# Making and broadcasting the gate rows at 38000 instead of 24000 of the plan's clock, in a fused attention and mixture kernel

## The chip, the cores and the metric

The kernel runs on one core of one Trainium2 chip. The metric is the time of one execution in device microseconds (us); before the change the median of three runs is 361.21 us.

## The reference

Two stages follow each other. Attention with four sink keys and a window of 128 keys runs over 4 batches, 8 heads, 768 positions of width 64. Its output, laid out as 3072 tokens of width 512, is the input of four experts, and every token goes through all of them, weighted by its gate:

```python
# _attn_ref, cut
scores = scale * np.matmul(q, k.transpose(0, 1, 3, 2))
keep = is_sink | in_window
a = softmax(np.where(keep, scores, -1e9))
x = np.matmul(a, v)            # -> (3072, 512)
# _moe_ref, cut
p = domain_probs / (domain_probs.sum(-1, keepdims=True) + 1e-09)
for e in range(E):
    h = np.maximum(x @ w1[e], 0.0)
    out += p[:, e:e + 1] * (h @ w2[e])
```

The shapes are w1 (4, 512, 1024), w2 (4, 1024, 512) and the probabilities (3072, 4).

## The kernel before, in words

**Tiles.** Each batch has three groups of 256 positions (g = 0, 1, 2). Attention goes by batch, group and head pair: transposes or DMA transposes of q and k, scores (L684), exponentials on ScalarE (L709), masks on VectorE (L718 in batch 0, L703 later), products with the values (L743 for the sinks, L750 for the window), a reciprocal and a scaling (L777, L780 or L789), and in batch 0 a transpose back (L808) into `xT`. The experts take `xT` group by group. A unit is (batch, group, expert).

**Two ways for a unit.** A slow unit has four steps of eight matmuls in its first layer (L1058). A fast one has seven products P1 to P7 of combined blocks (L1145), for which VectorE forms sums and differences of the weights (`vf` from w1 at L377 to L383, `wf` from w2 at L341 to L347) and of the tokens (L1114), and between the products VectorE and ScalarE combine partial results (L1191, L1198, L1204, L1213).

**Where the gates come in.** The units of batch 0's groups 0 and 1 are "early" units: ScalarE or VectorE evicts the first layer with a plain maximum (L1071, L1073), the second layer is L1397, and the gate is applied as one number for each token when VectorE evicts it (L1407, L1409). These numbers, `scale_t`, are made from the probabilities by `gates()` (L908 to L913), apart from the code changed here. Every later unit multiplies the gate in when its first layer is evicted (L1082 for slow units, L1178 for fast ones); there the tokens lie along the free dimension, so the gate must lie as a row, the same in all 128 partitions. The second layer of these units is L1319.

**Making the rows.** `gates_by_row()` (from L433) normalises the probabilities on VectorE with 24 partitions (L434 to L437), and SyncE (SP) stores the result in DRAM with two DMAs (L441). `load_gates()` (from L446) then lets SP broadcast rows from there to all partitions, 128 KB each, into at most NGATE = 5 buffers (L457): five at once, each further one when a buffer's unit is finished. The probabilities and the rows lie in `scratch` (L424), whose memory later takes `vf` of expert 2.

```python
    def gates_by_row():                                             # L433
        nc.vector.reduce_sum(out=ds, in_=dp, axis=AX.X)
        nc.vector.tensor_scalar_add(out=ds, in0=ds, scalar1=1e-9)
        nc.vector.reciprocal(out=ds, in_=ds)
        nc.vector.tensor_mul(
            pn, dp.rearrange("n p e -> n e p"), ds[:, None, :].to_broadcast([NT, E, P]),
        )
        for i in range(2):
            nc.sync.dma_start(out=gate_rows[:, :, i, :], in_=pn[i:NT:2])
        dve(2800, 0.0)
```

**What sets the order.** The instructions are issued by a planner that runs when the program is built. It keeps a clock for each engine in estimated ns (`t["pe"]`, `t["dve"]` and so on), and in each turn of its loop (L1455) emits the piece of TensorE work that is ready soonest or has the best priority; evictions and other work of VectorE and ScalarE wait in a list with due times and are emitted when their engine's clock allows. Every engine then carries out its own instructions in that order, and waits by semaphores for what they need. `now` is TensorE's clock. The call of the gate rows stands at the head of the loop, ahead of the turn's other emissions:

```python
        if not rowed and now > ROWED:                               # L1461
            rowed = 1
            gates_by_row()
            load_gates()
```

`dve(2800, 0.0)` puts the chain's estimate of some 3 us on VectorE's clock. The landing of a gate is in no clock of the planner. If no gate has been asked when the first gated unit opens, `emit_first` (L1033) asks for them itself; such units open only after attention of batch 0 is issued.

**The loads.** The weights of the four experts, 1 MB of DMA writes for each w1 and w2, and the rows of q, k and v go by GpSimd's (POOL's) queue, in the order of a list: w1 and w2 of expert 0, the last rows of batch 0, then w1 and w2 of experts 1 and 2, w1 of expert 3, rows of batch 1, w2 of expert 3 (L312, L322, L234, L299). SP's queue has the first loads, the gate rows, the DMA transposes (L246, L767) and the stores of the output.

Of the kernel before, what the change touches and what calls it, by code (L numbers as in the profile page):

```python
# [16 lines left out]
def kernel(  # L17
# [63 lines left out]
    OPEN = 2.2  # L81
    SOON = 21000
    NEARLY = 2
    ROWED = 24000
    W2AT = 2
    ROWS1 = 1500
    ONACT = 1
# [1367 lines left out]
    while mix.more() or att.more():  # L1455
        now = t["pe"]

        if not att.more() and ahead == B - 1 and not wide:
            wide = 1
            mix.widened()  # L1460
        if not rowed and now > ROWED:  # L1461
            rowed = 1
# [107 lines left out]
```

## Time and profile before

| | before |
|---|---|
| median of 3 runs | 361.21 us (360.98 to 362.25) |
| profiled execution, span | 361.5 us |
| around the span | nothing listed |
| TensorE (PE) busy | 351.5 us, 97% |
| VectorE (DVE) busy | 303.8 us, 84% |
| ScalarE (ACT) busy | 162.4 us, 45% |
| GpSimd (POOL) busy | 71.7 us, 20% |
| DMA moved | 37.79 MB, mean 105 GB/s |
| granted TensorE clock | 0.999 |
| gate chain on VectorE (L434) | starts at 24.9 us |
| first five gate broadcasts (L457) | issued from 34.7 us |
| first gated eviction (L1082) | 53.4 us |

The profile is one execution, so its rows are compared with its own span. Two kinds of line need a word. A line of a waits view names the engine and line that waited, what released it, and then total us, number of times and the longest. PE is TensorE's matmuls and PEld its weight loads, which overlap them. The DMA share of the page is full until about 135 us and low after that, so the first third of the run and the rest have different limits.

### The profile page before, as it was taken

What the parts mean: (1) busy time and instruction counts of PE and PEld (TensorE: products, weight loads), DVE (VectorE), ACT (ScalarE), POOL (GpSimd) and SP (SyncE); (2) the same over time, 40 slices, a digit from 0 to 9 for tenths busy, and PEclk for the clock granted to TensorE, in tenths of its full rate; (3) what the DMA queues carried; (4) which work ended last, traced back from release to release, by engine and by line L of the source; (5) the groups of instructions that cost most, each with busy time, mean ns of one, the idle gap of its engine ahead of it and who ended that gap; (6) DMA issues with size and microseconds to landing.
All of it is one profiled execution on the core that took longest, in us unless ns stands there. A gap on an engine that the chain in (4) does not pass through costs nothing.

```text
span 361.5 us, 10704 instructions
## 1 busy us (share of the span) xinstructions
PE 351.5 (97%) x4476; PEld 302.4 (84%) x4484; DVE 303.8 (84%) x691; ACT 162.4 (45%) x414; POOL 71.7 (20%) x92
## 2 busy tenths in 40 slices
PE   8999989998999999999999999999999999999995
PEld 3575758766789898898899898899899999999984
DVE  6787969868799899699579999989879799899840
ACT  5854722447694373554544435345344432313110
POOL 8936012540356224001071000000000000000000
PEclk9999999999999999999999999999999999999999
DMA  9999999999999999217099712121310131110011
GB/s 165 171 180 194 232 210 180 156 146 169 176 133 173 162 157 135 61 47 86 19 158 173 126 65 55 31 75 16 60 62 28 31 76 60 31 58 4 3 60 59
DMA packets 117869, 37.79 MB, mean 105 GB/s; under 512 B 100676, under 2 KB 113316, under 8 KB 117820
## 3 DMA queue, kind: packets, MB, share of 16 engines
q0 software_dynamic: 77520, 17.31, 54.0%
q1 hardware_dynamic: 39244, 19.28, 27.8%
q8 instruction: 35, 0.57, 0.6%
q10 hardware_dynamic: 1056, 0.52, 0.5%
q14 instruction: 14, 0.11, 0.1%
HBM read 40.98 MB, written 6.34 MB: 131 GB/s over the span
## 4 chain that ended last, share of the span: by engine, by line
PE 86%; DMA 11%; DVE 1%; issue 1%; ACT 1%; POOL 0%; ACTq 0%; POOLq 0%; DVEq 0%
PE acc L1319 34%; PE cps L1145 32%; DMA w<-in_moe_w_dram 9%; PE hps L1058 7%; PE acc L1397 6%; PE sps L684 3%; PE od L750 2%; DMA kraw<-in_k_dram 2%; PE od L743 1%; PE sinks L645 0%; ACT aT L709 0%; POOL w L312 0%; DVE qkn L345 0%; DVE qkn L343 0%; ACT qkn L270 0%
## 5 line engine op out<-in xcount | busy, mean ns | idle before, releaser
L1145 PEld LDWEIGHTS <-w 128*128 128x128 bf16 x1184 | 72.5, 98 | 2.3 <-issue 0.9
L1319 PEld LDWEIGHTS <-H 128*128 128x128 bf16 x700 | 65.0, 98 | 8.0 <-issue 1.5
L1178 DVE SCALAR_TENSOR_TENSOR H<-cps,gates 128x512 bf16<-128x512 f32 x90 | 60.3, 679 | 0.1
L709 ACT ACTIVATE aT<-sps 128x512 bf16<-128x512 f32 (+1 forms) x96 | 46.9, 573 | 24.7 <-PE sps L684 24.6
L1319 PE MATMUL acc<-w,H 128*128 128x256 bf16 x420 | 55.4, 273 | 0.0
L1145 PEld LDWEIGHTS <-vf 128*128 128x128 bf16 x744 | 45.6, 98 | 1.2 <-issue 0.5
L1145 PE MATMUL cps<-T,w 128*128 128x128 bf16 x592 | 45.0, 219 | 0.0
L1058 PE MATMUL hps<-xT,w 128*128 128x256 bf16 x352 | 43.3, 273 | 0.9 <-DMA w<-in_moe_w_dram 0.9
L1145 PE MATMUL cps<-xT,w 128*128 128x128 bf16 x592 | 43.7, 219 | 0.0
L789 ACT ACTIVATE onat<-od,R 128x64 bf16<-128x64 f32 x144 | 33.2, 323 | 22.7 <-DVE R L777 22.6
L1191 ACT COPY cps<-cps 128x512 f32<-128x512 f32 x37 | 21.4, 578 | 42.1 <-PE cps L1145 27.5
L1058 PEld LDWEIGHTS <-w 128*128 128x128 bf16 x352 | 33.3, 98 | 6.6 <-DMA w<-in_moe_w_dram 1.2
L1369 ACT COPY osb<-acc 128x256 f32<-128x256 f32 x36 | 13.6, 377 | 50.7 <-PE acc L1319 50.7
L1145 PE MATMUL cps<-T,vf 128*128 128x128 bf16 x496 | 36.4, 219 | 0.0
L299 POOL DMA_DIRECT2D vx<-in_v_dram x24 | 21.6, 905 | 62.2 <-PE od L750 48.5
L1319 PEld LDWEIGHTS <-S 128*128 128x128 bf16 x320 | 30.4, 98 | 3.3 <-issue 0.2
L1397 PE MATMUL acc<-w,H 128*128 128x512 bf16 x120 | 29.3, 379 | 2.0 <-DMA w<-in_moe_w_dram 1.3
L1198 DVE TENSOR_TENSOR cps<-H,cps 128x512 f32<-128x512 f32 x32 | 22.1, 691 | 9.8 <-PE cps L1145 8.4
L1319 PE MATMUL acc<-wf,H 128*128 128x256 bf16 x208 | 29.3, 273 | 0.0
L703 DVE TENSOR_TENSOR aT<-aT,mask 128x1024 bf16<-128x1024 bf16 (+1 forms) x36 | 22.7, 640 | 4.3 <-ACT aT L709 4.0
L1213 DVE TENSOR_TENSOR H<-H,cps 128x512 f32<-128x512 f32 x32 | 21.8, 680 | 2.7 <-PE cps L1145 2.6
L1397 PEld LDWEIGHTS <-H 128*128 128x128 bf16 x128 | 12.1, 98 | 13.5 <-issue 1.7
(128 smaller groups left out, 546.2 us busy)
## 6 DMA issues: line engine op xcount, KB each, us to landing
w<-in_moe_w_dram POOLq DMA_DIRECT2D x7, 1024.0 KB, 18.3
out_dram<-osb SPq DMA_DIRECT2D x21, 256.0 KB
gates<-gate_rows SPq DMA_DIRECT2D x40, 128.0 KB
vx<-in_v_dram POOLq DMA_DIRECT2D x24, 128.0 KB, 7.0
qkn<-in_q_dram POOLq DMA_DIRECT2D x22, 128.0 KB, 8.8
qkn<-in_k_dram POOLq DMA_DIRECT2D x22, 128.0 KB, 9.8
w<-in_moe_w_dram POOLq DMA_DIRECT2D x2, 512.0 KB, 9.4
kraw<-in_k_dram ACTq DMA_DIRECT2D x2, 256.0 KB
```

The costliest lines, as they stand in the source:

```text
L299: nc.gpsimd.dma_start(out=vx[tb][:, :, 0:D], in_=v[b, :, tb * P:(tb + 1) * P, :].rearrange("h p d -> p h d"),)
L703: nc.vector.tensor_mul(a, a, m[:, None, :].to_broadcast([P, 2, w]))
L709: nc.scalar.activation(out=a[:, ph], in_=sps[ph][:, 0:w], func=AF.Exp, scale=scale)
L789: nc.scalar.mul(o[:, qi, hp, ph * D:(ph + 1) * D], od[:, qi, ph, 0:D], R[:, qi, ph])
L1058: nc.tensor.matmul(h[:, i].rearrange("p (q n) -> p q n", q=2), lhsT=w1_sb[e][:, db, fb * P:(fb + 1) * P], rhs=xT[b, g][:, :, db], start=(i ...
L1145: nc.tensor.matmul(y[:, f], lhsT=A[:, d, f * P:(f + 1) * P], rhs=T[:, d], start=(m in ("P1", "P5") and f == 0 and d == 0), stop=(d == 1), ...
L1178: nc.vector.scalar_tensor_tensor(out=dst, in0=src, scalar=0.0, in1=gate, op0=ALU.max, op1=ALU.mult)
L1191: nc.scalar.copy(out=tiles["Y"], in_=y)
L1198: nc.vector.tensor_add(tiles["V"], c5, tiles["X"])
L1213: nc.vector.tensor_add(c5, c5, y)
L1319: nc.tensor.matmul(x, lhsT=self.operand(b, g, e, m)[:, f], rhs=forms[e][m][:, f], start=(k == 0 and f == 0 and m in (("P1", "P5", "P2") if ...
L1397: nc.tensor.matmul(op, lhsT=H[:, fb // QF, fb % QF, s], rhs=w2_sb[e][:, fb, :], start=(fb == 0), stop=(fb == NFB - 1),)
```

## The change

One constant of the planner changes. The gate rows are made, stored and broadcast in the first turn of the loop in which TensorE's clock has passed 38000 instead of 24000. No operation is added or removed by the edit itself; VectorE's clock gets the chain's estimate at the later point, and what the planner emits after either point may come in another order. In the trace of before the two stores are issued ahead of the DMAs that ask for expert 2's weights (28.8 and 29.7 us on POOL).

```diff
     OPEN = 2.2
     SOON = 21000
     NEARLY = 2
-    ROWED = 24000
+    ROWED = 38000
     W2AT = 2
     ROWS1 = 1500
     ONACT = 1
```

## The prediction

> **What bounds the kernel now.** I read four things in this order: the page's first part, the idle time of TensorE by cause, the timeline round the gates, and the DMA traffic in the same stretch.
>
> ```profile
> PE 351.5 (97%) x4476; PEld 302.4 (84%) x4484; DVE 303.8 (84%) x691; ACT 162.4 (45%) x414; POOL 71.7 (20%) x92
> ```
>
> TensorE is the bound: 351.5 of 361.5 us. Of the 10 us left, 3.3 lie in the first 20 us (busy 16.68) and 3.8 after 340 us (busy 17.75 of 21.5), mostly behind the last product. The waits of PE name what the edit can reach:
>
> ```profile
> PE acc L557 <- DVE lent L468: 1.4, 1, 1.4
> PE acc L1397 <- DMA w<-in_moe_w_dram: 1.3, 1, 1.3
> PE hps L1058 <- DMA w<-in_moe_w_dram: 0.9, 1, 0.9
> PE sinks L645 <- DVE qkn L345: 0.8, 1, 0.8
> ```
>
> The second is the one beside the gates: a second layer (L1397) waits for expert 1's w2. The timeline has both:
>
> ```profile
> 24.94 0.67 DVE L434 TENSOR_REDUCE scratch<-scratch 24x128 f32<-24x512 f32 x1
> 26.87 1.07 DVE L437 TENSOR_TENSOR scratch<-scratch 24x512 f32<-24x512 f32 x1
> 27.96 1.72 SPq L441 DMA_DIRECT2D gate_rows<-scratch  x2
> 34.66 2.28 SPq L457 DMA_DIRECT2D gates<-gate_rows  x5
> 46.21 1.89 PE L1397 MATMUL acc<-w,H 128*128 128x512 bf16 x7 [1.32 <-DMA w<-in_moe_w_dram]
> 53.36 0.69 DVE L1082 SCALAR_TENSOR_TENSOR H<-hps,gates 128x512 bf16<-128x512 f32 x1 [0.40 <-PE hps L1058]
> ```
>
> Columns: start, us, engine, line, operation; in brackets the idle time before. The chain of four DVE operations runs 24.94 to 27.94, the first broadcast is issued at 34.66, w2 of expert 1 is there at 46.17, and no gate is read before 53.36. The waits of SP's queue between 25 and 62 us give the latencies:
>
> ```profile
> SPq L457 <- DMA gate_rows<-scratch: 4.9, 1, 4.9
> SPq L457 <- DMA gates<-gate_rows: 3.1, 1, 3.1
> ```
>
> From DVE's end (27.94) to the first broadcast's issue is 6.7 us, 4.9 of them spent on the landing of the stores. The five issues end at 36.94, and 3.1 us later (40.07) the first gate is in: 5.4 us after its issue. The DMA answers for 35 to 38 us, 38 to 46 us and 46 to 53 us, in that order (packets, MB, share):
>
> ```profile
> q0 software_dynamic: 588, 0.62, 123.0%
> ...
> q0 software_dynamic: 832, 1.21, 83.3%
> q1 hardware_dynamic: 719, 0.66, 31.1%
> ...
> q0 software_dynamic: 1237, 1.46, 120.8%
> ```
>
> q0 carries the weights, q1 the broadcasts. Alone, q0 moves 0.62/3 = 0.207 and 1.46/7 = 0.209 MB per us; beside the gates 1.21/8 = 0.151. The gates take 8 x 0.208 - 1.21 = 0.45 MB of weights out of that stretch, 2.2 us of the stream.
>
> **The change part by part.** The plan's clock passed 24000 just before L434, at 24.94. It is TensorE's work that moves that clock, and TensorE idles about 0.4 us in the next 14, so 38000 falls near 24.9 + 14.0 + 0.4 = 39.3 us, between the masks and scalings (L718, L777, L780) of batch 0's last heads.
>
> *Taken away at 25 us:* 3.0 us of DVE and 1.7 us of SP issues. TensorE is busy 19.71 of 20 us there, and the DVE operation that followed (L910) waited 0.82 us for TensorE anyway. Gain: 0, at most 0.2.
>
> *Taken away between 32 and 46 us:* two 24 KB stores and five broadcasts. w2 of expert 1 lands 2.2 us earlier by the bytes: 44.0. By the landings: the weight before it landed at 22.48 + 15.2 = 37.7, and the last of the three after 46.17 at 30.53 + 30.6 = 61.1, so 5.0 each, which gives 37.7 + 5.0 = 42.7. TensorE asks at 46.21 - 1.32 = 44.89, perhaps a microsecond sooner in the new order. The whole wait goes: -1.3 us. What is late next: no wait of TensorE on a transfer follows it.
>
> *Put in at 39.3 us, DVE:* the chain, 0.67 + 0.21 + 0.94 + 1.07 with gaps, 3.0 us, until 42.3. Queued behind it are the remaining R, onat and mask operations of batch 0, and TensorE's L808 and L750 wait for those. The plan books the chain on its DVE clock, so it will put first-layer groups (L1058, evicted by ACT) there: five of 0.87 us run between 39.1 and 44.9, 4.4 us, more than 3.0. So 0 on TensorE. Without that cover it is up to 3.0, and the stretch has DVE idle for only 0.24 us of 39 to 46. The backlog runs on into 46 to 53.4, where DVE is busy 4.21 of 7.4 us: 3.2 idle, enough for 3.0. DVE thus comes to the first gated eviction at about 53.4, as before.
>
> *Put in at 42.3 us, SP:* two stores and then five broadcasts. SP issues nothing else between 8.4 and 60 us, so they are moved past nothing on SP. On POOL the loads of experts 2 and 3 and batch 1's first rows (28.79 to 38.8) are now asked ahead of them; they were queued without waiting for SP, so no issue moves. Repeating the latencies: 42.3 + 6.7 = 49.0 for the first broadcast, 49.0 + 5.4 = 54.4 for the first gate. The other four are wanted from 62.16 (L1178) on and follow over 6 us.
>
> *The wait that this adds:* L1082 has to wait until 54.4, from 53.4: +1.0 on DVE. Queued behind it are expert 2's forms (L377 to L383), the evictions L1409 and, from 59 on, the first fast units (L1198, L1178, L1213), whose next products wait for DVE. DVE idles 0.6 us in 53.4 to 60 and 0.1 in 60 to 67 (busy 6.90 of 7.00), so 1.0 - 0.6 = 0.4 us is left when the fast units run, and there TensorE can't be ahead of DVE: the 1.3 us gained at 45 are handed back, and it leaves this stage 0.4 us, say 0.3 for the last 0.1 idle, later than before. After 67 DVE has 3.5 us of slack in 13.
>
> No trace shows the latencies at the new place. The lower end takes the nearest shorter row for the stores' landing, 3.1 in place of 4.9 us: first gate at 52.6, in time, nothing added. The upper end is both latencies stretched by half, (6.7 + 5.4) x 1.5 = 18.2, first gate at 60.5. I take the measured sum, since weights fill q0 in both stretches alike (0.207 and 0.209).
>
> [...]
>
> *The buffer:* the probabilities lie where vf of expert 2 is written (L377, 53.97). The stores have read them by 49.0; 5 us of cover, cost 0.
>
> *The broadcasts at their new time* slow q0 by the same 2.2 us between about 52 and 61, after w2 of expert 2. What lands later than 61 is where it was. Cost 0.
>
> *The order after 45 us.* The plan redraws it, since its DVE clock differs. It can win at most the 0.8 us wait at 89 us: TensorE is busy 20.00 of 20 in every such window from 120 to 340. It can lose where DVE is full, 19.97 of 20 between 100 and 120: at most the 3.0 moved. I take 0, since the 3.5 us of DVE slack after 67 lie between.
>
> **The sum:** -1.3 + 1.6 (DVE's lag taking TensorE from 1.3 early to 0.3 late) = +0.3 us on the profiled 361.5. The page gives nothing around the span, which lies 0.3 above the runs' median of 361.21 and inside their 360.98 to 362.25; the same +0.3 on the median is 361.5.
>
> **The rivals.** (1) *The gates come in time.* For: 53.4 against 54.4 is one microsecond of difference in a sum of two latencies; against: both latencies were measured beside the same stream. Then the 1.3 us stay won: 359.9, and 359.1 where the 0.8 wait at 89 us goes too. [...]
>
> (2) *The gates are much too late, the slower side.* Place: the first L1082. Price: landing time less 53.4, less 0.7 us of DVE idle until 67. For: the broadcasts now meet the loads of batch 1's short rows, and DVE may enter the chain late, being full from 39 on. Against: the latencies above. It decides from a landing of 55.9 us on, where the loss reaches 1.8; at 57.5 it is 3.4: 364.6.
>
> (3) *The redrawn order pushes DVE work into 100 to 120 us.* For: no idle time there; against: the slack at 67 to 80. +1 to +3.0: 362.2 to 364.2.
>
> (4) *Nothing moves:* a fallback that loads gates when a unit opens could come first. Units open only after batch 0's attention is issued, behind 38000, so hardly: 361.2.
>
> **How the numbers follow.** This measurement can tell 0.5%, 1.8 us. My forecast (-0.6 to +1.4) has 0.42, rival 1 0.24, rival 2 0.18, rival 3 0.13, rival 4 0.03. Faster by more than 1.8 us needs rival 1 with its second wait: 0.10. Slower: all of rival 2, 0.09 of rival 3, 0.05 of the forecast's own upper tail: 0.32. Within: 0.58. The range goes from 359.7 (rival 1 with its one wait) to 364.3 (rival 2 almost to 57.5, and all of rival 3); outside lie about 0.12 below and 0.08 above.
>
> **What would show it.** L434 near 39 us, L441 near 42, L457 near 49; no wait of L1397 for a weight at 45 us; an idle of about 1 us on DVE ahead of the first L1082, put down to the gates' transfer, and TensorE pausing in L1145 at 60 to 67 us. Wrong if the gates are in before DVE asks, if L1397 still waits for its weight, or if TensorE has new idle time after 80 us.

## The result, and the profile after

The change makes the kernel slower: 364.45 us (median of five runs, 363.33 to 365.72) against 361.21 (five runs, 360.93 to 362.69), a ratio of 1.0079 with a 95% interval of 1.0054 to 1.0103, so by less than 1% but clear of the noise. The profiled execution has a span of 363.0 us and took 364.66 us, so 1.7 us lie around the span; the same 1.7 us stand in every later run.

The first part of the page of the changed kernel, engine, busy us, share and instructions, has hardly moved:

```profile
PE 352.8 (97%) x4475; PEld 303.8 (84%) x4483; DVE 303.8 (84%) x688; ACT 163.3 (45%) x417; POOL 71.5 (20%) x92
```

TensorE's busy time is 1.3 us more than in the first profile of before; a second profile of that kernel, below, has 352.5, so little of this is the change's. The waits of PE in the changed kernel (who waited, for what, total us, times, longest) have a new first line, and both waits for weights are gone:

```profile
PE cps L1145 <- DVE H L1082: 2.1, 1, 2.1
PE acc L557 <- DVE lent L468: 1.4, 1, 1.4
```

The timeline of the changed kernel shows the chain, the stores, the broadcasts and the first reader at their new places:

```profile
38.78 0.67 DVE L434 TENSOR_REDUCE scratch<-scratch 24x128 f32<-24x512 f32 x1
40.70 1.07 DVE L437 TENSOR_TENSOR scratch<-scratch 24x512 f32<-24x512 f32 x1
41.80 1.73 SPq L441 DMA_DIRECT2D gate_rows<-scratch  x2
43.07 1.89 PE L1397 MATMUL acc<-w,H 128*128 128x512 bf16 x7
47.84 14.61 SPq L457 DMA_DIRECT2D gates<-gate_rows  x6
55.16 0.69 DVE L1082 SCALAR_TENSOR_TENSOR H<-hps,gates 128x512 bf16<-128x512 f32 x1 [3.78 <-DMA gates<-gate_rows]
62.15 1.16 PE L1145 MATMUL cps<-T,vf 128*128 128x128 bf16 x16 [2.05 <-DVE H L1082]
```

L1397 has no bracket: expert 1's w2 was in at 40.93 by the landing records, 5.2 us sooner than in the profile of before. Not all of that is the gates' doing. The trace has sixteen landing records of this transfer; in the profile of before fifteen are in by 42.62 and the last only at 46.17, and expert 2's two weights behind it have a like lag of 2.7 and 2.6 us in their last record. A second profile of before, below, has w2 in at 43.81. Ahead of L1082 VectorE sits idle for 3.78 us, put down to the gates' transfer; from 60.10 on, 5 us after it starts, TensorE pauses for 2.05. The stores took 41.80 to 47.8, 6.0 us, and the broadcast 47.84 to 55.06, 7.2. SP's queue, from 25 to 62 us, waits 4.3 us for the stores (4.9 before) and, with its five issues done, 5.0 for the first gate (3.1 before):

```profile
SPq L457 <- DMA gates<-gate_rows: 5.0, 1, 5.0
SPq L457 <- DMA gate_rows<-scratch: 4.3, 1, 4.3
```

The chain of the changed kernel, cut to 38 to 64 us (start, us, what), runs from the chain on VectorE through both transfers to the product that paused:

```profile
40.70 1.07 DVE scratch L437
...
42.76 5.02 DMA gate_rows<-scratch
...
47.84 7.23 DMA gates<-gate_rows
...
55.16 0.13 DVE H L1082
...
62.15 1.91 PE cps L1145 x23
```

In the DMA traffic of the changed kernel (packets, MB, share) the first line is 38 to 46 us, where q0 moved 1.21 MB before; the other two are 53 to 60 us, where the broadcasts on q1 now lie:

```profile
q0 software_dynamic: 1139, 1.66, 115.7%
...
q0 software_dynamic: 4174, 0.90, 141.9%
q1 hardware_dynamic: 593, 0.53, 28.6%
```

So the weights did get their stretch back: 1.66 MB in 8 us is the undisturbed 0.208 per us. It bought no time, as the experiments show.

The windows of the changed kernel hold one more thing. Columns: window, length, busy us and count of PE, PEld, DVE, ACT, POOL, then the granted TensorE clock:

```profile
60.00:62.00 2.00, 0.10 (x2) 0.00 (x0) 2.00 (x4) 0.57 (x1) 1.83 (x3) 1.00 2.24 166
62.00:64.00 2.00, 1.85 (x25) 1.84 (x25) 2.00 (x5) 0.58 (x1) 1.79 (x3) 0.74 1.36 203
64.00:66.00 2.00, 2.00 (x22) 2.00 (x21) 1.83 (x4) 0.60 (x1) 1.21 (x2) 0.50 1.22 214
66.00:68.00 2.00, 2.00 (x35) 2.00 (x34) 1.95 (x4) 0.60 (x2) 0.00 (x0) 0.91 1.34 199
```

From 0.8 us after the pause the clock stands at half for 3.41 us (from 62.96 by the clock's records). The third window has 22 products; the same window of a later profile of this kernel at full clock (e6, below) has 34. Half of 3.41 is 1.7 us of TensorE's time.

### The profile page after: what moved, and what is told of

It reads as the page before. It is cut to its first block, busy times and chain, and to the rows that moved or that the text cites. A ratio compares the mean times of both kernels' runs of the same rounds, so it can differ in the third digit from the quotient of the medians.

```text
span 363.0 us, 10702 instructions
## 1 busy us (share of the span) xinstructions
PE 352.8 (97%) x4475; PEld 303.8 (84%) x4483; DVE 303.8 (84%) x688; ACT 163.3 (45%) x417; POOL 71.5 (20%) x92
## 4 chain that ended last, share of the span: by engine, by line
PE 84%; DVE 6%; DMA 5%; ACT 2%; issue 1%; POOL 1%; DVEq 0%; SPq 0%; ACTq 0%
PE acc L1319 33%; PE cps L1145 31%; PE hps L1058 8%; PE acc L1397 5%; PE sps L684 3%; PE od L750 2%; DMA gates<-gate_rows 2%; DMA gate_rows<-scratch 1%; DMA vx<-in_v_dram 1%; ACT aT L709 1%; PE od L743 1%; DVE onat L780 1%; DVE H L1082 1%; DVE H L1178 1%; DVE aT L718 1%
## 5 line engine op out<-in xcount | busy, mean ns | idle before, releaser
L1145 PEld LDWEIGHTS <-w 128*128 128x128 bf16 x1184 | 73.7, 99 | 2.3 <-issue 0.9
L1145 PEld LDWEIGHTS <-vf 128*128 128x128 bf16 x744 | 46.0, 98 | 4.0 <-issue 3.4
L1145 PE MATMUL cps<-T,w 128*128 128x128 bf16 x592 | 46.0, 221 | 0.0
L1145 PE MATMUL cps<-xT,w 128*128 128x128 bf16 x592 | 44.1, 220 | 0.0
L1058 PE MATMUL hps<-xT,w 128*128 128x256 bf16 x352 | 42.9, 273 | 0.0
L1145 PE MATMUL cps<-T,vf 128*128 128x128 bf16 x496 | 36.3, 219 | 2.5 <-DVE H L1082 2.1
L1058 PEld LDWEIGHTS <-w 128*128 128x128 bf16 x352 | 33.4, 98 | 5.0 <-issue 0.6
L1397 PE MATMUL acc<-w,H 128*128 128x512 bf16 x120 | 29.2, 379 | 0.6 <-issue 0.3
L1397 PEld LDWEIGHTS <-H 128*128 128x128 bf16 x128 | 12.1, 98 | 12.1 <-issue 0.2
```

Of the source, the lines that this page charges most:

```text
L1058: nc.tensor.matmul(h[:, i].rearrange("p (q n) -> p q n", q=2), lhsT=w1_sb[e][:, db, fb * P:(fb + 1) * P], rhs=xT[b, g][:, :, db], start=(i ...
L1145: nc.tensor.matmul(y[:, f], lhsT=A[:, d, f * P:(f + 1) * P], rhs=T[:, d], start=(m in ("P1", "P5") and f == 0 and d == 0), stop=(d == 1), ...
L1397: nc.tensor.matmul(op, lhsT=H[:, fb // QF, fb % QF, s], rhs=w2_sb[e][:, fb, :], start=(fb == 0), stop=(fb == NFB - 1),)
```

## The experiments

Theory A was the prediction's own account with the measured latencies: the late gates cost more than foreseen, while w2 wins 1.3 us back. Theory B, formed after the first four runs, says that the wait for w2 was never part of the usual execution. A third candidate was the redrawn issue order. Ratios are against the kernel before, run on the same chip.

**One half of the change alone (e1_split).** The rows are made and stored at 24000 as before; only the broadcasts come at 38000. A small write by VectorE into each new buffer goes with it.

```diff
+        x = mo.tile(...); len(gate_sb) < NGATE and nc.vector.memset(x[:, 0, 0:1], 0.0)
...
             gates_by_row()
-            load_gates()
+        if rowed == 1 and now > 38000: rowed = 2; load_gates()
```

> The chain and the stores stay at 24000, and every engine keeps its order of before; only the first five broadcasts are held back until 38000, by five one-column memsets on VectorE that they have to wait for. Theory (the landing of the gates decides): broadcasts issued near 39.5 us, first gate in near 45, expert 1's w2 in by 43 to 44, so neither the wait of L1397 at 45 us nor a wait of L1082 for a gate: 359.5 to 360.0, faster than before by 1.2 to 1.7 us. Rival (the redrawn order, not the landing, made the change slow, and the weight's wait is not the gates' doing): as before, 361.2, with the wait of L1397 still there.

Measured: 362.11 us, ratio 1.0013 [0.9989, 1.0037]. The first gate was in at 44.58, w2 at 42.53, L1397 did not wait, the first L1082 ran at 51.03 without waiting for a gate. The conditions of a gain of 1.3 us were all met, and no gain came. Four of the ten runs had a mean granted clock of 0.995 and took 363.7 to 363.9 us; the other six took 361.3 to 362.2, level with the 361.86 of before and not 1.3 below it. The longest wait that the edit could have caused is 1.8 us of L645 for a DMA transpose at about 87 us, where the kernel before, run again below, waits 1.0; so up to 0.8 us of a gain could hide there, not the whole.

**The order of before, the chain late (e2_plan_of_before).** The planner's clock is charged at 24000 as before, and chain, stores and broadcasts are issued at 38000, unbooked.

```diff
-        dve(2800, 0.0)
...
-            gates_by_row()
-            load_gates()
+            dve(2800, 0.0)
+        if rowed == 1 and now > 38000: rowed = 2; gates_by_row(); load_gates()
```

> The chain, the stores and the broadcasts stand at 38000 as in the change, but the plan books them at 24000, so all other work keeps its order of before. Theory (landing): first gate in near 55 us as in the change; VectorE comes to L1082 later than in the change (near 53.4 instead of 51.4), so it waits 1 to 2 us instead of 3.8, and TensorE also waits up to 2 us near 40 to 45 because nothing was planned to cover the chain: 361.5 to 363.5. Rival (the redrawn order is what costs): back to 359.8 to 361.2.

Measured: 364.24 us, ratio 1.0049 [1.0031, 1.0067]; chain at 39.91, stores 42.9, broadcasts 48.98, first gate 54.76. Here the chain itself stops TensorE, as its timeline shows:

```profile
43.48 0.28 PE L808 MATMUL tx<-ident,onat 128*128 128x128 bf16 x2 [2.61 <-DVE onat L780]
```

The first L1082 comes only at 55.43 and waits 0.40 us for its own product, not for a gate, so theory A's wait of 1 to 2 us there did not come. Of the 4.4 us that it is later than in the kernel before (51.00 in the second profile, below), 2.6 are this hold-up; 1.7 are a wait of L1058 for a weight near 20 us, ahead of the chain, which belongs to this execution and not to the edit. The 3.0 us of chain thus hold TensorE up by 2.6 where the plan does not book them. In the change, where it does, TensorE's longest wait for L780 is 0.2, since it has first-layer products to do, as a line of the changed kernel's timeline shows:

```profile
38.71 4.53 PE L1058 MATMUL hps<-xT,w 128*128 128x256 bf16 x40
```

So the cover by first-layer groups is real, and the change pays at the gates instead. In time the hold-up of e2 comes to less than 2.6: the four other runs at a clock of 1.0 took 362.9 to 363.3 us, 1.0 to 1.4 above before, and the five at 0.995 took 364.1 to 364.6.

**The first gate not loaded (e3_first_gate_set).** The change, but GpSimd sets the first buffer to 1.0 where SP would load it, which leaves out the gating of that one unit and 128 KB of broadcast; the order on VectorE and TensorE is that of the change.

```diff
-        nc.sync.dma_start(
+        nc.gpsimd.memset(x, 1.0) if not gate_sb else nc.sync.dma_start(
```

> The changed kernel, but the gate of the first gated unit (batch 0, group 2, expert 0) is a constant 1 set by GpSimd instead of a broadcast, so that unit's gating is left out; all else, the order on VectorE and TensorE included, is that of the change. Theory (landing): L1082 starts near 51.4 without waiting, TensorE has no idle near 60, its clock does not drop, and the time is below before: 359.0 to 360.2. Rival (redrawn order, or the chain standing between the masks): stays at 363 to 364.5.

Measured: 361.83 us, ratio 0.9997 [0.9984, 1.001]. In its timeline the first gated eviction has no bracket:

```profile
51.13 0.69 DVE L1082 SCALAR_TENSOR_TENSOR H<-hps,gates 128x512 bf16<-128x512 f32 x1
```

One landing taken away takes the whole loss away, with the redrawn order still in place. That rules out the order as its cause, and it gives VectorE's arrival in the changed kernel: 51.1, not 53.4. It fell back to the kernel before, though, not below it, where theory A had it.

**The point halfway (e4_rowed31000, e7_rowed34000).** One constant each.

```diff
-    ROWED = 24000
+    ROWED = 31000   # e7: 34000
```

> The constant at 31000, half way. Theory (landing): chain on VectorE near 32 us, first broadcast issued near 42, gates in from 47 to 54, all before they are read (51 and 60 us on), and expert 1's w2 in before 44: both waits gone, 359.0 to 360.2. Rival (redrawn order costs by itself): 362 to 364.

Measured: 361.84 us, ratio 0.9999 [0.9983, 1.0016]. The first gate was in at 47.98; L1082 at 51.53 waited for its product alone. The conditions of theory A's gain were met again, and again no gain came.

> The constant at 34000. Theory (the first gate's landing against the first L1082 sets the loss, microsecond for microsecond beyond a slack): chain from about 35 us, first broadcast issued near 44, first gate in near 50 to 51, L1082 asks for it at 51: a wait of 0 to 0.5 us, time as before, ratio 0.998 to 1.002. Rival (the loss grows steadily with the distance that the chain is moved, whatever lands when): two thirds of the change's loss, ratio about 1.004.

Measured: 362.04 us, ratio 1.0004 [0.9986, 1.0021]; first gate at 50.01, L1082 at 51.31, no wait for it, as the landing theory had it; a loss in step with the distance moved, 1.004, is outside the interval.

**The kernel before, profiled again (e0_before_again).** No edit.

> The kernel before once more, for a second profile of it. Theory A (the wait of L1397 for expert 1's w2 belongs to every run of before): that wait is there again, 1 to 1.5 us at 45 us, and the span is 361.5 as in the first profile. Theory B (it was that one execution: the w2 came late there and usually comes in time): no such wait, w2 in by 44 to 45, and a span of 359.7 to 360.4.

Measured: 361.77 us, ratio 1.0002 [0.9984, 1.0019], span 360.0. Three lines of its timeline:

```profile
51.00 0.69 DVE L1082 SCALAR_TENSOR_TENSOR H<-hps,gates 128x512 bf16<-128x512 f32 x1 [0.40 <-PE hps L1058]
67.93 0.75 DVE L1409 SCALAR_TENSOR_TENSOR osb<-acc,scale_t,osb 128x512 f32<-128x512 f32 x1 [0.92 <-PE acc L1397]
87.22 0.29 PE L645 MATMUL sinks<-qkT,ksd 128*32 128x256 bf16 x4 [0.98 <-DMA qkT<-qkn]
```

No wait for a weight stands in its list; w2 of expert 1 was in at 43.81 and L1397 ran at 43.85. The first gated eviction is at 51.00, where the first profile has 53.36. That profile, with a span of 361.5, took some 363.2 us with the 1.7 around it, more than any of the five runs that were timed. Theory B holds as far as two profiles can tell: the waits of 1.3 and 0.9 us are not in every execution. Such waits for weights come and go: the L1058 that waited 0.9 us near 20 us waited 0.34 in e1's profile and 1.70 in e2's. Against e0 the changed kernel's w2 comes 2.8 us sooner (41.01 in e6), near the 2.2 that the prediction had by the bytes; but in e0 TensorE comes to L1397 just after w2 is in, so there is no wait to win.

**The change again (e6_change_again).** No edit to the changed kernel.

> The changed kernel once more beside the same runs of before, for a second profile. Theory (landing): L1082 waits 3.5 to 4 us for its gate again, TensorE pauses 2 to 2.6 us near 59 to 62, and the time is 362.9 to 364.7; where the clock does not drop the span is 361.6 to 362.2, where it drops it is up to 364. Rival: the wait of L1082 varies by more than a microsecond between executions, and the time with it.

Measured: 363.61 us (363.35 to 364.62), ratio 1.0053 [1.0033, 1.0074], span 361.6 at a clock of 0.999. The same three places:

```profile
54.70 0.69 DVE L1082 SCALAR_TENSOR_TENSOR H<-hps,gates 128x512 bf16<-128x512 f32 x1 [3.75 <-DMA gates<-gate_rows]
71.06 0.75 DVE L1409 SCALAR_TENSOR_TENSOR osb<-acc,scale_t,osb 128x512 f32<-128x512 f32 x1 [0.58 <-PE acc L1397]
89.30 0.29 PE L645 MATMUL sinks<-qkT,ksd 128*32 128x256 bf16 x4
```

Set against e0 they give the account of the loss: +3.7 us at the first gate, +3.1 at L1409, +2.1 at L645, and +1.6 at the end (361.6 against 360.0). The first step down, 3.7 to 3.1, is idle time that VectorE had. Another microsecond and a half is swallowed behind it, since the kernel before waits there anyway: 0.98 us at L645 for batch 1's transposes, which SP issues from 75.59 on there and from 76.01 on here, and 0.31 and 0.26 us in L1145 near 98 and 100 us. TensorE is busy 18.45 of 20 us between 80 and 100 in e0, and 20.00 of 20 in e6.

**The pause filled (e5_fill).** The change with nine products of 512 columns on zeros ahead of the fast product that waits for VectorE, at the same 2.05 us.

```diff
+            ; [nc.tensor.matmul(acc[self.turn % 2], lhsT=zeros[:, 0:P], rhs=zeros, start=True, stop=True) for _ in range(9 * ((b, g, e, m) == (0, 0, 2, 'P5')))]
```

> The changed kernel with nine products of 512 columns on zeros (1.9 us of TensorE at full clock, into an accumulator that is free) placed right ahead of the product that waits 2.05 us near 60 us; the plan does not book them and the rest is the change. Theory (part of the loss is TensorE's clock, which fell to half for 3.4 us after that wait): no drop of the clock, 0.5 to 1.7 us less than the change, 362.0 to 363.5. Rival (the drop has another cause, or costs nothing because VectorE sets the pace there): the time of the change, 363.9 to 364.5, or more if the products delay it.

Measured: 363.72 us (363.53 to 363.86), ratio 1.0053 [1.0032, 1.0074]; the clock is 0.999 or 1.0 in every run, and L1082 waits 3.71 us as in the change. Its windows have TensorE busy where e6 had 0.31 us:

```profile
60.00:62.00 2.00, 1.89 (x10) 0.78 (x8) 2.00 (x5) 0.57 (x1) 1.25 (x2) 1.00 2.40 157
```

The spread shrinks to 0.33 us, and the median stays where e6 has it, between the two expectations and in neither. So the loss does not need the halved clock; the late gate makes it. The slower executions of the change are those with the lower clock: 363.33 us at 0.999 against 364.45 and 364.66 at 0.995 in the first measurement, so about a microsecond of the 1.7 comes out in the time. Three of the five runs there have such a clock (0.995 or below) and one of the six of e6, which fits the ratios 1.0079 and 1.0053. That the filling prevents the drop is not shown, since five of e6's six runs have none either.

**Later still (e8_rowed41000).** ROWED at 41000.

> The constant at 41000. Theory (landing): chain from about 42 to 43 us, first broadcast near 51.5, first gate in near 58.5, so L1082 waits about 7 to 7.5 us instead of 3.75, and all of the added 3 to 3.5 us comes out in the time: 366.5 to 367.5, ratio 1.013 to 1.016, a little more where TensorE's clock drops. Rival (loss grows with the distance moved, 1.0053 for 14000): ratio 1.006 to 1.007.

Measured: 365.68 us (365.34 to 365.97), ratio 1.0097 [1.007, 1.0124]. First gate in at 57.51; its timeline has the wait on both engines:

```profile
57.61 0.69 DVE L1082 SCALAR_TENSOR_TENSOR H<-hps,gates 128x512 bf16<-128x512 f32 x1 [6.41 <-DMA gates<-gate_rows]
58.35 1.03 PE L1058 MATMUL hps<-xT,w 128*128 128x256 bf16 x8 [3.06 <-DVE H L1082]
```

The clock fell to half for 3.41 us in the profiled execution (from 60.40), and the mean clocks of all four runs, 0.994 to 0.995, fit the same in each. The ratio lies between the two expectations, so neither was met: the wait was 6.4 us instead of the 7 to 7.5 that theory A's sum had, and again the stretch up to 100 us took back 1.5 to 2 us. By the profiles the reader came 2.9 us later than in e6 and the end 2.5 us later; how much of this the halved clock adds was not separated.

The first gate's landing against the reader's 51.0 orders these points of the constant: at 47.98 and 50.01 nothing is lost, at 54.6 to 55.06 some 2 to 3 us, at 57.51 3.6.

**Half the bytes (e9_gates_bf16, e10_bf16_31000, e11_bf16_again).** The kernel before with the rows, their store and their broadcasts in bf16, which rounds the gates to that type; e10 has ROWED at 31000 with it, e11 repeats e9.

```diff
-    pn = scratch[0:NT, 4 * P:8 * P].rearrange("n (e p) -> n e p", e=E)
+    pn = scratch[0:NT, 10 * P:12 * P].bitcast(BF16).rearrange("n (e p) -> n e p", e=E)
-    gate_rows = dram.tile([NT // 2, E, 2, P], FP32, name="gate_rows")
+    gate_rows = dram.tile([NT // 2, E, 2, P], BF16, name="gate_rows")
-        x = mo.tile([P, 2, P], FP32, name="gates", tag="gates", bufs=NGATE)
+        x = mo.tile([P, 2, P], BF16, name="gates", tag="gates", bufs=NGATE)
```

> The kernel before with the gate rows stored and broadcast in bf16, half the bytes (64 KB instead of 128 KB a broadcast, 0.45 MB less before 75 us); order and plan unchanged. Theory (behind the gates lies a floor set by the transfers: TensorE waits near 87 us for batch 1's transposes, and that wait swallowed a part of the change's loss): the loads behind the broadcasts come 1 to 2 us sooner, the wait at 87 us shrinks by about a microsecond, ratio 0.996 to 0.999. Rival (that wait is set by SyncE's own order or by the straggling DMA engine, not by bytes): 1.000.

> Gate rows in bf16 and the constant at 31000, the two variants that did no harm put together. Theory (fewer bytes are worth about a microsecond, and a landing ahead of the first L1082 costs nothing): as the bf16 rows alone, ratio 0.996 to 0.998. Rival (the bf16 gain hangs on the order of 24000): 0.999 to 1.001.

> Gate rows in bf16 at 24000 once more, beside the same runs of before. Theory (a real gain of the fewer bytes): ratio 0.996 to 0.998 again, with less idle time of TensorE near 87 us than the kernel before's 2.0 us of pauses between 80 and 100 us. Rival (the first ratio was the luck of that series): 0.999 to 1.001.

Measured: 360.82 us, ratio 0.9972 [0.9955, 0.9989]; 360.85, 0.9967 [0.995, 0.9985]; 361.12, 0.997 [0.9952, 0.9988]. The three agree on about a microsecond, and each beats both kernels. Where it comes from is open: at L645 the profile of e9 still waits 0.77 us and that of e11 1.42, and only e10's has no wait there. The shorter pause that was expected between 80 and 100 us did not show in e11: TensorE is idle 1.9 us there, 1.55 in e0.

## Why the prediction was right and wrong

The way in which the change costs time is the forecast's: the gates land too late, VectorE waits at the first L1082, and TensorE pauses behind it. The size was missed, by one term that does not exist and one that was too small. The forecast was 361.5 us, and 364.45 came, just above the range of 359.7 to 364.3; put on the 361.21 of before, the ratio gives 364.1, just inside. The range reached so far only by rivals 2 and 3, neither of which came about as described, so it is luck that the result lies near its end. The likeliest outcome, within 1.8 us (0.58), did not come; slower by more (0.32) did.

**Places of the moved steps.** Near: L434 at 38.8 (39.3 foretold), the stores at 41.80 (42.3), the first broadcast at 47.84 (49.0), the first gate in at 55.06 and, in e6, 54.6 (54.4). The two latencies were 6.0 and 7.2 us instead of 6.7 and 5.4, 13.2 against 12.1 in sum. That the landing came out within 0.7 us is in part luck: a chain 0.5 early and stores 0.7 short offset a broadcast 1.8 longer, whose last part of sixteen came at 55.06, 1.5 after the fifteenth.

**Cost 0 for the chain.** Right, and for the reason given: e2 shows 2.6 us without the booking, the change none.

**"The whole wait goes: -1.3 us."** The wait did go, and w2 came in at 40.93, sooner than the 42.7 to 44.0 foretold. The term failed as a gain. It was a stall of one profiled execution: e0 has none, and e1, e3, e4 and e7, all without waits for w2 and for the gate, tie with the kernel before. The term is 0. The reading by the landings set the 8.5 us from the weight before to this one against the usual 5.0; 2 of the 8.5 are last landing records, 1.5 us late there and 3.5 here. The warning was in the figures: the span of 361.5 was set 0.3 above the median of 361.21, as if nothing lay around it; with the 1.7 us that do, that execution was 2 us slower than the median, about the sum of its two waits for weights, which e0 has not.

**"DVE thus comes to the first gated eviction at about 53.4."** This is the term that decided. 53.36 came from the same delayed execution; e0 has 51.00 and e3, in the changed order, 51.13. The wait was therefore 3.75 to 3.78 us and not 1.0, although the landing was foretold to within 0.7 us. The idle time of VectorE that the prediction set against it, 0.6 to 0.7 us, was right: 3.7 us at the reader became 3.1 at L1409 in e6, where the prediction had 1.0 become 0.4.

**"What is late next: no wait."** Partly wrong, and it softened the loss. Batch 1's transposes were a floor at 87 us that the kernel before ran into; 1.0 of the 3.1 us vanishes there and 0.5 by 100 us. The prediction saw the 0.8 us at L645 and booked it only as something to be won. And TensorE's pause in L1145, foretold at 60 to 67 and found at 60.1 to 62.15, had a follower that was not foreseen: the halved clock.

**The rivals.** Rival 1 fell, since the gates are late. Rival 2, gates much too late, is the nearest in size, but for another reason than the one it needed: the landing stayed below its threshold of 55.9, and the reader was earlier. Rival 3, the redrawn order, is ruled out by e3. Rival 4 did not occur.

## What to carry to other kernels

A stall that one profile shows may not be in the next execution of the same program. Before its removal is booked, compare the profiled time, span and surroundings together, with the timed runs, and take a second profile: here it moved both the gain (1.3 to 0) and the reader's arrival (53.4 to 51.0). A step that ends in a store and a broadcast has its deadline set by the landing, and this chain took 15 to 16 us from its start to the first landing (3.0 on VectorE, 6 to 7 and 5 to 7 for the transfers beside a full weight stream), which no clock of the planner knew. With less than that ahead of the first reader, the lateness comes out in the time, here less some 2 us of idle time and waits that were there anyway.

## What the runs showed of the hardware that was not expected

In two profiles TensorE's granted clock halved after a short pause. Behind 2.05 us (with 0.40 just before) it stood at half for 3.41 us in the profiled execution of the change, and the same pause in e6 left it whole. Behind 2.61 us in the profile of e2 it stayed whole too, though five of e2's ten runs had a mean clock of 0.995, what one such drop would leave (1.7 us lost of some 362). Behind e8's 3.06 and 0.82 us it fell in the profile, and the mean clock fits a drop in every run. Both drops were 3.41 us long. What brings one about is not shown: the same 2.05 us were followed by it in one execution and not in another.

The latency of the same broadcast, from issue to landing, was not the same at each place in the run: it took 5.1 us in e4 and e7, 5.4 in the profile of before, 6.0 in e8 and 7.2 in the changed kernel, which is 2 us more than the shortest for the same bytes. Its sixteen parts need not land together: in the changed kernel the last came 1.5 us after the fifteenth, in the profile of before 0.35, in e4 and e7 within 0.1 us. Why is not shown.
